# First dense matrix by seven block products per pair of token blocks, its weights' factors made in three steps per unit

## The chip, the cores and the metric

The kernel runs on one core of a Trainium2 chip. The metric is device time in microseconds (us), taken as the median of the runs. The profile is of one execution; its span runs from the first instruction to the last.

## What is computed

Three layers run one after the other, all in fp32: retention (linear attention with decay) over 8 batches, 8 heads and 576 positions; a mixture of 8 experts, one expert for each of the 4608 tokens; and a dense pair of matrices with a squared ReLU between them. The change lies in the third layer and in the making of its weights, which takes place during the second.

```python
def _moe_ref(x, w_gate, w1, w2):            # x: 4608 x 512
    logits = x @ w_gate                     # 512 x 8
    expert_idx = np.argmax(logits, axis=1)
    ...
    for e in range(E):
        mask = expert_idx == e
        h = np.maximum(x[mask] @ w1[e], 0.0)        # 512 x 1024
        out[mask] = gate_w[mask, None] * (h @ w2[e])  # 1024 x 512

def _moe2_ref(x, w_in, w_out):              # w_in 512 x 2048, w_out 2048 x 512
    h = x @ w_in
    r = np.maximum(h, 0.0)
    g = r * r
    return (g @ w_out).astype(np.float32)
```

The dense weights arrive as float64, which the kernel reads as pairs of 32-bit words.

## The kernel before, in words

**Precision.** Every product of the expert and the dense layer is made of three matmuls: each operand is split into a high part (rounded to the TensorE's fp32r format by a ScalarE copy) and a low part (the rest, by a VectorE subtraction), and high x high, high x low and low x high are added up in PSUM.

**Expert stage.** Work goes in 64 units `u = 8 e + f`: expert `e`, slice `f` of 128 hidden features. A unit is `first(u)`, 24 matmuls of 320 token slots in two parts (L712 to L714), each with a ScalarE ReLU into `hh` and a VectorE op into `hl` (L718, L719), and `second(u)`, 15 matmuls of 512 columns (L736 to L738). TensorE runs `first(u+1)` and then `second(u)`. The two parts use three PSUM banks in turn (`l1_ps`). VectorE and ScalarE also split each unit's weights six units ahead (`split_unit`, L97 and L98, on GpSimd for one unit in eight), turn the next expert's gathered tokens (`transp`, L684 to L689), and make the dense weights: `split_wide` reads 512 float64 columns of one dense slice (`craw`), builds the fp32 value with integer ops, splits it into `cw` (two buffers), and two units later SP stores `cw` to the DRAM tensor `wd_d`. 32 such jobs run at five in eight units. At unit 18 `rest_of` branches on whether any expert has more than 640 tokens; the branch is not taken with these inputs.

**End of the expert stage.** The last six units' `second` run tile by tile, and after each tile `finish` scatters its rows to `y_d`, from which `fetch` reads the tokens of dense block 0 again.

**Dense stage.** Nine blocks of 512 tokens. For each block and each of 16 slices of 128 hidden features, `up` is 12 matmuls of 512 columns into one PSUM bank (L937), `squares` is ReLU, square, split (L942 to L948), and `down` is 12 matmuls into four accumulators (L958 to L960). `up` runs two slices ahead of `down`. All 16 slices of weights (`w<-wd_d`) are loaded once and stay in SBUF. Block 0 starts with half a block (256 columns) while its other tokens arrive. The four accumulators leave through four output tiles.

**Order.** Nothing is scheduled automatically: each engine runs its instructions in the order in which the code issues them, and SP issues nearly all DMAs from one queue in order.

Of the kernel before, what the change touches and what calls it, by code (L numbers as in the profile page):

```python
# [19 lines left out]
NT = 36  # L20
NE = 8
# [6 lines left out]
REST = 18  # L28
# [3 lines left out]
GROUPS = [(0, 8), (8, 16), (16, 24), (24, 30), (30, 36)]  # L32

# [4 lines left out]
def body(ctx, tc, att, tab_v, tab_x, masks, wg, ident, pick, cst, wu, wd, out):  # L38
# [80 lines left out]
    def split_wide(j, raw):  # L119
        v, s = divmod(j, 2)  # L120
        low, high = raw[:, :, 0], raw[:, :, 1]
        m = pools["cv_p"].tile([128, 512], F32, tag="cm", name="cm")
        x = pools["cv_p"].tile([128, 512], F32, tag="cx", name="cx")
        t = pools["cv_p"].tile([128, 512], I32, tag="ct", name="ct")
        a = pools["cv_p"].tile([128, 512], F32, tag="ca", name="ca")
# [9 lines left out]
            out=a.bitcast(I32), in0=xi, scalar=-0x40000000, in1=t, op0=ALU.bitwise_and, op1=ALU.bitwise_or  # L135
        )
        vec.tensor_scalar(
            out=m.bitcast(I32), in0=a.bitcast(I32), scalar1=-0x800000, scalar2=None, op0=ALU.bitwise_and
        )
        vec.scalar_tensor_tensor(  # L140
            out=x, in0=low.bitcast(U32), scalar=2.0 ** -52, in1=m, op0=ALU.mult, op1=ALU.mult
        )
        w = pools["cw_p"].tile([128, 2, 512], F32R, tag="cw", name="cw")
        act.activation(out=w[:, 0], in_=a, func=AF.Copy)
        vec.tensor_tensor(out=a, in0=a, in1=w[:, 0].bitcast(F32), op=ALU.subtract)
        vec.tensor_tensor(out=w[:, 1], in0=a, in1=x, op=ALU.add)
        return lambda: sp.dma_start(out=wd_d[v, :, :, 512 * s:512 * s + 512], in_=w.bitcast(F32))

    def load_dense(v, wpool):
        w = wpool.tile([128, 2, 1024], F32R, tag="w", name="w")  # L150
        sp.dma_start(out=w.bitcast(F32), in_=wd_d[v])
        w_q[NE * 8 + v] = w
# [91 lines left out]
    w_q = {}  # L244

# [6 lines left out]
    with ExitStack() as es:  # L252
# [253 lines left out]
        def lead_rows():  # L506
# [18 lines left out]
        raw = {}  # L525
        lead_x = [
            pools["cw_p"].tile([128, 2, 512], F32R, tag="cw", name=f"lead{s}").rearrange(
                "p s (k n) -> p (s k) n", n=128 * LEAD
            ) for s in range(2)
# [30 lines left out]
        for t in range(NT):  # L560
# [39 lines left out]
            if t % 6 == 2 and 12 <= t < 36:  # L600
                w_q[t // 6 - 2] = split_unit(t // 6 - 2, raw.pop(t - 2), pool)
# [4 lines left out]
        for v, tags in ((4, ("ct", "ca")), (5, ("cm", "cx"))):  # L606
            halves[v] = [pools["cv_p"].tile([128, 512], F32, tag=t, name="half") for t in tags]
# [483 lines left out]
```

## Time and profile before

| | before |
|---|---|
| median of 3 runs | 1433.29 us (1427.59 to 1435.78) |
| profiled execution | 1436.04 us, span 1434.2 us |
| PE busy | 97% of the span |
| first dense matmul | at 644.4 us |
| granted clock, mean | 0.991 |

PE is TensorE, DVE VectorE, ACT ScalarE, POOL GpSimd, SP the queue that issues DMAs. A busy PE is a union of overlapping matmuls, so its pace is read from counts over a stretch.

### The profile page before, as it was taken

The page shows a single profiled execution, that of the slowest core. Times are in us where ns is not written, and L with a number is a line of the kernel's source. Part 1 is how long each engine was busy: PE and PEld are TensorE (multiplying, and loading weights), DVE is VectorE, ACT ScalarE, POOL GpSimd, SP SyncE. Part 2 cuts the span into 40 slices and gives each one's busy share as a digit, 9 for nine tenths or more (in the row PEclk, how much of TensorE's full clock was granted, in tenths as well). Part 3 has the DMA queues.
Part 4 walks back from the last instruction along what each step waited for, and adds up shares of the span by engine and source line. Part 5 has one row for each costly group of instructions (what it writes and reads, how often), then busy time and mean ns, then how long its engine had stood idle before and what let it go on. Part 6 is the DMA issues. An engine that isn't in the chain of part 4 may idle for free.

```text
span 1434.2 us, 20323 instructions
## 1 busy us (share of the span) xinstructions
PE 1391.3 (97%) x8217; PEld 1192.2 (83%) x8217; DVE 712.5 (50%) x1187; ACT 435.3 (30%) x764; POOL 313.2 (22%) x277
## 2 busy tenths in 40 slices
PE   7989799998999999999999999999999999999998
PEld 5777688887999999998888888888888888888887
DVE  5667656886888888723323233232333323333222
ACT  1212233443444444422222222222222222222221
POOL 2223246765657557310000000000000000000000
PEclk9999999999999999999999999999999999999999
DMA  8999744765756757538120020200102020020000
GB/s 309 293 298 303 210 131 135 241 226 176 234 186 222 227 185 237 189 134 312 81 59 0 1 59 0 59 1 27 33 0 59 1 57 3 0 59 1 30 0 30
DMA packets 92406, 172.51 MB, mean 120 GB/s; under 512 B 16654, under 2 KB 54030, under 8 KB 86672
## 3 DMA queue, kind: packets, MB, share of 16 engines
q1 hardware_dynamic: 82944, 151.03, 33.3%
q0 software_dynamic: 9360, 20.10, 4.3%
q8 instruction: 66, 1.08, 0.3%
q14 instruction: 36, 0.29, 0.1%
HBM read 125.86 MB, written 46.28 MB: 120 GB/s over the span
## 4 chain that ended last, share of the span: by engine, by line
PE 72%; issue 3%; DMA 1%; POOL 0%; SPq 0%; ACT 0%; POOLq 0%; DVE 0%
PE fl L937 27%; PE fa L959 9%; PE fa L958 9%; PE fa L960 9%; PE l L712 3%; PE l L713 3%; PE l L714 3%; PE acc L737 3%; PE acc L736 3%; PE acc L738 3%; DMA w<-wd_d 1%; DMA y_d<-y,sidx 0%; POOL y_d L227 0%; SPq L633 0%; DMA yi<-y_d 0%
## 5 line engine op out<-in xcount | busy, mean ns | idle before, releaser
L937 PE MATMUL fl<-xt,w 128*128 128x512 f32 (+1 forms) x1776 | 415.3, 383 | 1.5 <-DMA w<-wd_d 1.5
L937 PEld LDWEIGHTS fl<-xt,w 128*128 128x128 f32 x1776 | 327.1, 188 | 67.3 <-issue 1.9
L944 DVE TENSOR_TENSOR fr<-fr 128x512 f32<-128x512 f32 x144 | 99.8, 693 | 401.2 <-ACT fr L942 401.2
L958 PE MATMUL fa<-w,gh 128*128 128x512 f32 x576 | 224.1, 389 | 0.0
L959 PE MATMUL fa<-w,gh 128*128 128x512 f32 x576 | 224.1, 389 | 0.0
L960 PE MATMUL fa<-w,gl 128*128 128x512 f32 x576 | 224.1, 389 | 0.0
L942 ACT ACTIVATE fr<-fl 128x512 f32<-128x512 f32 x144 | 86.2, 599 | 416.0 <-PE fl L937 416.0
L206 POOL DMA_INDIRECT xs<-x_d,qidx x140 | 154.0, 1100 | 44.4 <-issue 42.4
L712 PE MATMUL l<-xt,w 128*128 128x320 f32 (+1 forms) x480 | 150.2, 313 | 8.8 <-DVEq L759 6.2
L713 PE MATMUL l<-xt,w 128*128 128x320 f32 (+1 forms) x480 | 149.8, 312 | 0.0
L948 DVE TENSOR_TENSOR gl<-fr,gh 128x512 fp32r<-128x512 f32 x144 | 99.8, 693 | 100.6 <-ACT gh L946 100.6
L714 PE MATMUL l<-xt,w 128*128 128x320 f32 (+1 forms) x480 | 149.7, 312 | 0.0
L958 PEld LDWEIGHTS fa<-w,gh 128*128 128x128 f32 x576 | 108.1, 188 | 22.5
L959 PEld LDWEIGHTS fa<-w,gh 128*128 128x128 f32 x576 | 108.2, 188 | 22.3
L960 PEld LDWEIGHTS fa<-w,gl 128*128 128x128 f32 x576 | 108.0, 188 | 22.4
L736 PE MATMUL acc<-w,hh 128*128 128x512 f32 x320 | 125.7, 393 | 0.0
L737 PE MATMUL acc<-w,hh 128*128 128x512 f32 x320 | 125.3, 392 | 0.0
L738 PE MATMUL acc<-w,hl 128*128 128x512 f32 x320 | 124.8, 390 | 0.1
L946 ACT ACTIVATE gh<-fr 128x512 fp32r<-128x512 f32 x144 | 91.0, 632 | 109.7 <-DVE fr L944 109.7
L712 PEld LDWEIGHTS l<-xt,w 128*128 128x128 f32 x480 | 90.7, 189 | 12.1 <-issue 6.6
L713 PEld LDWEIGHTS l<-xt,w 128*128 128x128 f32 x480 | 90.7, 189 | 2.4 <-DVE xt L689 0.2
L714 PEld LDWEIGHTS l<-xt,w 128*128 128x128 f32 x480 | 90.7, 189 | 0.0
(140 smaller groups left out, 1511.4 us busy)
## 6 DMA issues: line engine op xcount, KB each, us to landing
raw<-wu SPq DMA_DIRECT2D x62, 512.0 KB, 4.0
in<-att SPq DMA_DIRECT2D x28, 1024.0 KB, 7.9
craw<-wd SPq DMA_DIRECT2D x32, 512.0 KB, 5.6
wd_d<-cw SPq DMA_DIRECT2D x32, 512.0 KB, 6.7
w<-wd_d SPq DMA_DIRECT2D x16, 1024.0 KB, 16.4
x_d<-xr SPq DMA_DIRECT2D x144, 64.0 KB, 5.4
yi<-y_d SPq DMA_DIRECT2D x32, 256.0 KB, 6.0
out<-fo SPq DMA_DIRECT2D x32, 256.0 KB, 2.8
```

What stands on the lines that cost most here:

```text
L206: pool.indirect_dma_start(out=xs, out_offset=None, in_=src, in_offset=bass.IndirectOffsetOnAxis(ap=index, axis=0),)
L712: pe.matmul(ps, w[:, 0, k], hi[:, k, cs], start=(k == 0), stop=False)
L713: pe.matmul(ps, w[:, 0, k], lo[:, k, cs], start=False, stop=False)
L714: pe.matmul(ps, w[:, 1, k], hi[:, k, cs], start=False, stop=(k == 3))
L736: pe.matmul(acc[i], hh[:, cs], w[:, 0], start=(f == 0), stop=False)
L737: pe.matmul(acc[i], hh[:, cs], w[:, 1], start=False, stop=False)
L738: pe.matmul(acc[i], hl[:, cs], w[:, 0], start=False, stop=(f == 7))
L937: pe.matmul(ps, w[:, s, k], x[:, k, ts], start=(n == 0), stop=(n == 11))
L944: vec.tensor_tensor(out=gg, in0=r, in1=r, op=ALU.mult)
L958: pe.matmul(acc[i], gh[:, cs], w[:, 0], start=(f == 0), stop=False)
L959: pe.matmul(acc[i], gh[:, cs], w[:, 1], start=False, stop=False)
L960: pe.matmul(acc[i], gl[:, cs], w[:, 0], start=False, stop=(f == 15))
```

## The change

The dense layer's first matrix is taken in blocks of two by two. Tokens go in pairs of blocks and the 512 input features in two halves of 256, so that each product of a pair with 256 hidden features is four blocks wide, and seven products of half the inner length replace eight. A product `up(T, j, i, n)` is six matmuls instead of two times twelve for a block of 128 features and two token blocks: per pair `T` and per `j` (8 of them, 256 hidden features each) seven products in the order `ORDER` fill three kinds of PSUM bank. Products 7, 3, 2 and 6 add on top of what a bank already holds, and `keep`, `block` and the subtractions in `up` combine the seven. Block 0 is alone, so its two halves form the first pair (`T = 0`, 256 columns per matmul); blocks 1 and 2, 3 and 4, 5 and 6, 7 and 8 form the others (512 columns). All `up` of a pair come first; then `halve` splits the stored squares and `down` runs, one block of the pair after the other.

The left factors (sums of weight blocks, split high and low) are made in the expert stage: per `j` six jobs, one per unit from unit 5 to 52: two `narrow`, two `left_factors`, two `split_wide`. Each job has three steps in its unit: before `first`, after it, and at the start of the next unit. `cw` has one buffer, twice as large. The right factors (sums of token blocks) are made by `factor`, for `T = 0` on VectorE at the start of the dense stage, for later pairs on GpSimd, ScalarE and VectorE during the `down` of the pair before. Weights no longer stay in SBUF: `stream` loads 1 MB tiles of `ws_d` through a ring of four buffers, 22 tiles for `T = 0` and 30 for each other pair. `split_unit` goes to GpSimd for two units in eight. `rest_of` moves from unit 18 to the end of the loop over units.

```diff
+LEFT = [
+    (1, "11", ALU.add, "22"), (2, "21", ALU.add, "22"), (3, "11", None, None), (4, "22", None, None),
+    (5, "11", ALU.add, "12"), (6, "21", ALU.subtract, "11"), (7, "12", ALU.subtract, "22"),
+]
+RIGHT = [
+    (1, "11", ALU.add, "22"), (2, "11", None, None), (3, "12", ALU.subtract, "22"), (4, "21", ALU.subtract, "11"),
+    (5, "22", None, None), (6, "11", ALU.add, "12"), (7, "21", ALU.add, "22"),
+]
+ORDER = [5, 1, 4, 7, 3, 2, 6]
+KEPT = [5, 1, 7, 4, 2, 6, 3]
...
-    pools["cw_p"] = scope(early, "cw_p", 2, side="right")
+    pools["cw_p"] = scope(early, "cw_p", 1, side="right")
...
-    wd_d = dram.tile([NF, 128, 2, 1024], F32, name="wd_d")
+    ws_d = dram.tile([22, 128, 4, 512], F32, name="ws_d")
...
+    def narrow(raw, tag, made):
+        t, m, x = words(raw)
+        yield
+        low_word(raw, m, x)
+        a = pools["cv_p"].tile([128, 512], F32, tag=tag, name=tag)
+        vec.tensor_tensor(out=a, in0=t, in1=x, op=ALU.add)
+        made.append(a)
+        yield
...
+    def split_wide(v, raw):
+
+        t, m, x = words(raw)
+        yield
+        w = pools["cw_p"].tile([128, 4, 512], F32R, tag="cw", name="cw")[:, 0:2]
+        act.activation(out=w[:, 0], in_=t, func=AF.Copy)
+        low_word(raw, m, x)
+        yield
+        vec.tensor_tensor(out=t, in0=t, in1=w[:, 0].bitcast(F32), op=ALU.subtract)
+        vec.tensor_tensor(out=w[:, 1], in0=t, in1=x, op=ALU.add)
+        yield lambda: sp.dma_start(
+            out=ws_d[14 + v // 2, :, 2 * (v % 2):2 * (v % 2) + 2], in_=w.bitcast(F32)
+        )
...
+    def left_factors(j, x0, x1, part):
+
+        blk = {"11": x0[:, 0:256], "12": x0[:, 256:512], "21": x1[:, 0:256], "22": x1[:, 256:512]}
+        these = KEPT[0:4] if part == 0 else KEPT[4:7]
+        n = len(these)
+        yield
+        sums = pools["cv_p"].tile([128, 3, 512], F32, tag="cv", name="sums").rearrange("p a (b n) -> p (a b) n", n=256)
+        w = pools["cw_p"].tile([128, 4, 512], F32R, tag="cw", name="cw").rearrange("p k (s n) -> p k s n", s=2)
+        s = blk[LEFT[these[-1] - 1][1]]
+        act.activation(out=w[:, n - 1, 0], in_=s, func=AF.Copy)
+        for m, i in enumerate(these[:-1]):
+            _, a, op, b = LEFT[i - 1]
+            vec.tensor_tensor(out=sums[:, m], in0=blk[a], in1=blk[b], op=op)
+        act.activation(out=w[:, 0:n - 1, 0], in_=sums[:, 0:n - 1], func=AF.Copy)
+        yield
+        vec.tensor_tensor(out=w[:, n - 1, 1], in0=s, in1=w[:, n - 1, 0].bitcast(F32), op=ALU.subtract)
+        vec.tensor_tensor(
+            out=w[:, 0:n - 1, 1], in0=sums[:, 0:n - 1], in1=w[:, 0:n - 1, 0].bitcast(F32), op=ALU.subtract
+        )
+        k = 7 * j + 4 * part
...
+    stream_of = [t for T in range(5) for t in (*range(14), *(range(14, 22) if T == 0 else 2 * [*range(14, 22)]))]
+
+    def stream(on):
+
+        n = len(ring_q)
+        w = on.tile([128, 4, 2, 256], F32R, tag="w", name="wq")
+        sp.dma_start(out=w.rearrange("p k s n -> p k (s n)").bitcast(F32), in_=ws_d[stream_of[n]])
+        ring_q.append(w)
...
+    def factor(i, x1, x2, hi, lo, cs, on=None):
+
+
+        _, a, op, b = RIGHT[i - 1]
+        blk = {"11": x1 and x1[:, 0:2], "21": x1 and x1[:, 2:4], "12": x2 and x2[:, 0:2], "22": x2 and x2[:, 2:4]}
+        s = blk[a]
+        if b:
+            s = xf_p.tile([128, 2, 128], F32, tag="xs", name="xsum")
+            (on or pool).tensor_tensor(out=s, in0=blk[a], in1=blk[b], op=op)
+        parts = [
+            (h[:, :, cs], l[:, :, cs], s[:, ks])
+            for ks, h, l in zip((slice(0, 2),) if len(hi) == 1 else (slice(0, 1), slice(1, 2)), hi, lo)
+        ]
+        for h, l, s in parts:
+            act.activation(out=h, in_=s, func=AF.Copy)
+
+        def rest():
+            for h, l, s in parts:
+                vec.tensor_tensor(out=l, in0=s, in1=h.bitcast(F32), op=ALU.subtract)
+
+        return rest
...
+        def first_of_them(order, x1, x2):
+            rest = None
+            for i, t in order:
+                r = factor(i, x1[t], x2[t], [x0_c[i, 0]], [x0_c[i, 1]], slice(128 * t, 128 * t + 128), vec)
+                if rest:
+                    rest()
+                rest = r
+            rest()
...
+        work = [(what, j, r) for j in range(8) for what, r in (
+            ("in", 0), ("in", 1), ("sum", 0), ("sum", 1), ("out", 0), ("out", 1))]
...
+            job, rests = None, []
+            if last_job:
+                f_ = next(last_job)
+                if f_:
+                    f_()
+                last_job = None
...
+                rests.append(split_unit(v, raw.pop(v), pool if f in (5, 6) else vec))
+            if 5 <= u < 5 + len(work):
+                what, j, r = work[u - 5]
+                if what == "in":
+                    job = narrow(wide.pop(0), ("ca", "cb")[r], made)
+                elif what == "sum":
+                    job = left_factors(j, *made[2 * j:], r)
+                else:
+                    job = split_wide(2 * j + r, wide.pop(0))
...
+            for f_ in rests[:1]:
+                f_()
+            if job:
+                next(job)
+            for f_ in rests[1:]:
+                f_()
...
+                next(job)
+                last_job = job
...
-                if u == REST:
-                    rest_of()
...
+        rest_of()
+        for _ in range(2):
+            stream(w_a)
...
+                first_factors()
...
+        bank_of = {5: "b5", 1: "b1", 4: "b4", 7: "b1", 3: "b5", 2: "b4", 6: "b5"}
+        bank_ps = {"b1": b1_ps, "b4": b4_ps, "b5": b5_ps}
+        steps = [(None, 0)] + [(2 * n - 1, 2 * n) for n in range(1, 5)]
...
+            terms = [(c, a, b) for c in range(2) for a, b in ((0, 0), (0, 1), (1, 0))]
+            for m, (c, a, b) in enumerate(terms):
+                pe.matmul(
+                    ps, w[:, a, c], xc[T][i, b][c], start=(i in (5, 1, 4) and m == 0), stop=(m == 5),
+                    skip_group_check=True,
+                )
...
+            def block(b, ps, s):
+                o = g[b][:, j, 0:n]
+                if s is None:
+                    act.activation(out=o, in_=ps, func=AF.Relu)
+                    act.activation(out=o, in_=o, func=AF.Square)
+                else:
+                    vec.tensor_tensor(out=o, in0=ps, in1=s, op=ALU.add)
+                    vec.scalar_tensor_tensor(out=o, in0=o, scalar=0.0, in1=o, op0=ALU.max, op1=ALU.mult)
+
+            if i in (5, 1, 4):
+                keep(f"s{i}", j, ps, n)
+                if all((f"s{m}", j) in sums for m in (5, 1, 4)):
+                    vec.tensor_tensor(out=at("s4"), in0=at("s4"), in1=at("s5"), op=ALU.subtract)
+                    vec.tensor_tensor(out=at("s1"), in0=at("s1"), in1=at("s4"), op=ALU.add)
+                    if j in cut and not cut.discard(j):
+                        vec.tensor_tensor(out=at("s1"), in0=at("s1"), in1=bank("b4"), op=ALU.subtract)
...
+            elif i == 7:
+                block("11", ps, at("s4"))
+            elif i == 3:
+                block("12", ps, None)
+            elif i == 2:
+                block("21", ps, None)
+                if ("s1", j) in sums:
+                    vec.tensor_tensor(out=at("s1"), in0=at("s1"), in1=ps, op=ALU.subtract)
+                else:
+                    cut.add(j)
+            else:
+                block("22", ps, at("s1"))
...
+        def halve(T, h, f):
+
+            hi, lo = [pools["cg_p"].tile([128, 512], F32R, tag=f"c{s}", name=f"c{s}") for s in "hl"]
+            if T:
+                parts = [(g["12"[f % 2] + "12"[h]][:, f // 2], slice(0, 512))]
+            else:
+                parts = [(g["12"[f % 2] + "12"[s]][:, f // 2, 0:256], slice(256 * s, 256 * s + 256)) for s in range(2)]
+            for s, o in parts:
+                act.activation(out=hi[:, o], in_=s, func=AF.Copy)
+                vec.tensor_tensor(out=lo[:, o], in0=s, in1=hi[:, o].bitcast(F32), op=ALU.subtract)
+            cg[T, h, f] = hi, lo
...
+                o = pools["cg_p"].tile([128, 512], F32, tag="o", name="fo")
...
+        head = [(0, "up", j, i) for i, j in (
+            (4, 0), (4, 1), (4, 2), (2, 0), (2, 1), (2, 2), (4, 3), (2, 3),
+            (5, 0), (5, 1), (1, 0), (1, 1), (7, 0), (7, 1), (3, 0), (3, 1), (6, 0), (6, 1),
+        )]
+        slots = []
+        for T in range(5):
+            slots += [(T, "up", j, i) for j in range(8) for i in ORDER if (T, "up", j, i) not in head]
+            slots += [(T, "down", h, f) for h in range(2 if T else 1) for f in range(16)]
...
+        for T, _, j, i in head[:8]:
+            up(T, j, i, 256)
+        x2 = [turn(yi[0][:, 2], x0_p)]
+        order = [(5, 0), (1, 0), (7, 0), (5, 1), (1, 1), (7, 1), (3, 0), (3, 1), (6, 0), (6, 1)]
+        first_of_them(order[:3], x0_t, x2)
+        x2.append(turn(yi[0][:, 3], s_p, "s5"))
+        first_of_them(order[3:], x0_t, x2)
+        for T, _, j, i in head[8:]:
...
+                if T < 4 and b == 6 and a in (4, 5):
+                    if a == 4:
+                        load, jobs = prepare(T + 1)
+                    load(a - 4)
...
+                for _ in range(2 if T else 3):
+                    if jobs:
+                        jobs.pop(0)()
+            t = tile_of(T, what, a, b)
+            left[t] -= 1
+            if left[t] == 0 and t >= 4 and t + 4 < len(stream_of):
+                stream(w_a)
         for i in (0, 1, 3, 2):
```

Place 1: ScalarE in the expert stage, over about one unit. `w<-raw` is the high part of a unit's weights, `hh<-l` the ReLU of `first`, `cw` the high part of a dense factor, `cm<-craw` and `cv<-craw` the first step of reading float64. Before:

```order
L126 ACTIVATE cm<-craw 128x512
L144 ACTIVATE cw<-ca 128x512
L97 ACTIVATE w<-raw 128x1024
L718 ACTIVATE hh<-l_5445 128x320
L718 ACTIVATE hh<-l_5460 128x320
L126 ACTIVATE cm<-craw 128x512
L144 ACTIVATE cw<-ca 128x512
```

After:

```order
L808 ACTIVATE hh<-l_3137 128x320
L808 ACTIVATE hh<-l_3152 128x320
L176 ACTIVATE cw<-cv 128x512
L112 ACTIVATE w<-raw 128x1024
L778 ACTIVATE xt_3031<-xf 128x4x128
L140 ACTIVATE cv<-craw 128x512
L808 ACTIVATE hh<-l_3207 128x320
L808 ACTIVATE hh<-l_3222 128x320
L176 ACTIVATE cw<-cv 128x512
```

The copy into `cw` keeps its place behind the two ReLUs, but it now stands in each of four units in six, always on the same buffer.

Place 2: ScalarE where the dense stage begins; `xt` are the token operands' high parts, `fr`/`gh` the squares before, `s` and `g` the kept products and squares after. Before:

```order
L655 ACTIVATE xt_8041<-yf 128x4x128 x2
L747 ACTIVATE y<-acc_7755,gg 128x512
L655 ACTIVATE xt_8041<-yf 128x4x128
L655 ACTIVATE xt_8041<-yf 128x2x128 x2
L942 ACTIVATE fr<-fl_8160 128x512
L946 ACTIVATE gh<-fr 128x512
```

After (the end of the first eight products, and what follows):

```order
L1113 ACTIVATE g_8194<-b_8218 128x256
L1114 ACTIVATE g_8194<-g_8194 128x256
L1085 ACTIVATE s_8225<-b_8251 128x256
L1113 ACTIVATE g_8194<-b_8251 128x256
L1114 ACTIVATE g_8194<-g_8194 128x256
L739 ACTIVATE xt_8142<-yf 128x2x128
L739 ACTIVATE xt_8143<-xsum 128x2x128 x2
```

Before, the copies of the later tokens stand ahead of the first product's ReLU; now the copies of the later tokens (`xt<-yf`, `xt<-xsum`, the last two rows) stand behind all results of the first eight products.

Place 3: SP's queue from the end of the expert stage; `yi` and `yq` are the tokens of the dense blocks. Before:

```order
L151 DMA w<-wd_d 128x2048 x4
L633 DMA yi<-y_d 32x8x128 x4
L633 DMA yi<-y_d 32x4x128 x8
L633 DMA yi<-y_d 32x16x128 x4
L151 DMA w<-wd_d 128x2048 x12
L979 DMA out<-fo 128x512 x4
```

After:

```order
L317 DMA wq<-ws_d 128x2048 x2
L707 DMA yi<-y_d 32x4x128 x16
L317 DMA wq<-ws_d 128x2048 x6
L707 DMA yq<-y_d 32x4x128 x8
L317 DMA wq<-ws_d 128x2048 x2
L707 DMA yq<-y_d 32x4x128 x8
L317 DMA wq<-ws_d 128x2048 x4
```

The twelve loads of weights that stood in one row behind the tokens are now a ring, with the tokens of the next pair between its tiles, eight DMAs at a time.

## Rows read from the trace of the kernel before

**Rows 1.** The page's first part, of the whole span: busy us (share) xinstructions

```profile
PE 1391.3 (97%) x8217; PEld 1192.2 (83%) x8217; DVE 712.5 (50%) x1187; ACT 435.3 (30%) x764; POOL 313.2 (22%) x277
```

**Rows 2.** Windows in the dense stage: PE busy, PEld, DVE, ACT, POOL, clock, DMA share, GB/s

```profile
644.40:650.20 5.80, 5.80 (x50) 5.80 (x49) 2.94 (x6) 2.06 (x4) 0.98 (x1) 1.00 0.16 48
...
663.00:1420.00 757.00, 757.00 (x3340) 627.01 (x3341) 244.28 (x358) 199.15 (x326) 0.00 (x0) 1.00 0.12 35
```

**Rows 3.** Groups by form, PE, whole span: xcount | busy us, mean ns | idle before

```profile
L937 PE MATMUL fl<-xt,w 128*128 128x512 f32 x1680 | 403.6, 389 | 1.5 <-DMA w<-wd_d 1.5
...
L937 PE MATMUL fl<-xt,w 128*128 128x256 f32 x96 | 11.7, 283 | 0.0
```

**Rows 4.** Waits of PE, whole span: total us, times, longest

```profile
PE l L712 <- DVEq L759: 6.2, 1, 6.2
...
PE fl L937 <- DMA w<-wd_d: 1.5, 1, 1.5
```

**Rows 5.** Timeline, PE, one unit of the expert stage: start us, us

```profile
543.87 0.30 PE L712 MATMUL l<-xt,w 128*128 128x320 f32 x1
...
550.81 0.30 PE L712 MATMUL l<-xt,w 128*128 128x320 f32 x1
```

**Rows 6.** Groups by form, DVE, 400 to 600 us

```profile
L98 DVE TENSOR_TENSOR w<-raw,w 128x1024 fp32r<-128x1024 f32 x25 | 30.5, 1220 | 6.7 <-ACT w L97 6.4
L719 DVE SCALAR_TENSOR_TENSOR hl<-l,hh 128x320 fp32r<-128x320 f32 x58 | 26.5, 483 | 7.8 <-ACT hh L718 7.8
...
L127 DVE SCALAR_TENSOR_TENSOR cx<-cm,craw 128x512 f32<-128x512 f32 x18 | 12.4, 687 | 0.6
...
L137 DVE TENSOR_SCALAR cm<-ca 128x512 int32<-128x512 int32 x18 | 7.9, 436 | 0.6
```

**Rows 7.** The same of ACT

```profile
L144 ACT ACTIVATE cw<-ca 128x512 fp32r<-128x512 f32 x18 | 11.4, 635 | 41.5 <-issue 41.5
```

**Rows 8.** Source L147, the store of a dense factor: its last line

```profile
DMA to landing us min/median/max: 3.1/6.7/10.0
```

**Rows 9.** Windows of the twelve loads of dense weights, columns as in rows 2

```profile
665.00:670.00 5.00, 5.00 (x24) 4.13 (x23) 1.39 (x2) 1.23 (x2) 0.00 (x0) 1.00 1.01 419
```

**Rows 10.** Windows at the leftover branch, columns as in rows 2

```profile
326.00:334.00 8.00, 2.04 (x9) 1.34 (x8) 1.63 (x4) 2.35 (x4) 6.02 (x7) 0.78 0.79 248
334.00:340.00 6.00, 5.79 (x28) 5.69 (x29) 3.18 (x5) 1.68 (x4) 4.62 (x5) 0.73 0.48 149
```

**Rows 11.** Timeline, DVE, where the expert stage ends

```profile
641.37 1.31 DVE L648 STREAM_TRANSPOSE yf<-yi 128x512 f32<-128x512 f32 x2
...
648.16 0.77 DVE L648 STREAM_TRANSPOSE yf<-yi 128x256 f32<-128x256 f32 x2 [0.93 <-DMA yi<-y_d]
```

**Rows 12.** Groups by form, DVE, 640 to 1434 us

```profile
L944 DVE TENSOR_TENSOR fr<-fr 128x512 f32<-128x512 f32 x144 | 99.8, 693 | 401.2 <-ACT fr L942 401.2
...
L656 DVE TENSOR_TENSOR xt<-yf,xt 128x256 fp32r<-128x256 f32 x2 | 0.8, 422 | 0.2 <-ACT xt L655 0.2
```

**Rows 13.** The same of ACT

```profile
L946 ACT ACTIVATE gh<-fr 128x512 fp32r<-128x512 f32 x144 | 91.0, 632 | 109.7 <-DVE fr L944 109.7
...
L655 ACT ACTIVATE xt<-yf 128x256 fp32r<-128x256 f32 x2 | 0.7, 417 | 2.1 <-DVE yf L648 2.1
```

**Rows 14.** Timeline, SP's queue, dense stage

```profile
741.53 2.71 SPq L633 DMA_DIRECT2D yi<-y_d  x4
```

**Rows 15.** DMA issues, whole span: xcount, KB each, median us to landing

```profile
out<-fo SPq DMA_DIRECT2D x32, 256.0 KB, 2.8
...
yi<-y_d SPq DMA_DIRECT2D x8, 64.0 KB, 2.0
```

**Rows 16.** Timeline, DVE, beside a GpSimd split

```profile
411.10 0.69 DVE L689 TENSOR_TENSOR xt<-xf,xt 128x512 fp32r<-128x512 f32 x1 [0.70 <-ACT xt L688]
...
415.26 1.92 DVE L689 TENSOR_TENSOR xt<-xf,xt 128x512 fp32r<-128x512 f32 x1 [0.70 <-ACT xt L688]
```

**Rows 17.** Timeline, POOL, the same stretch

```profile
414.23 2.40 POOL L98 TENSOR_TENSOR w<-raw,w 128x1024 fp32r<-128x1024 f32 x1 [3.63 <-ACT w L97]
```

More of the change, by code (lines that the diff above doesn't have):

```diff
@@ L27 @@
 FIN = 6
-REST = 18
 LEAD = 2
@@ L140, in split_wide, with low_word @@
+    def low_word(raw, m, x):
         vec.scalar_tensor_tensor(
-            out=x, in0=low.bitcast(U32), scalar=2.0 ** -52, in1=m, op0=ALU.mult, op1=ALU.mult
+            out=x, in0=raw[:, :, 0].bitcast(U32), scalar=2.0 ** -52, in1=m, op0=ALU.mult, op1=ALU.mult
         )
[L143 to L146, printed above, removed]
@@ L600, in body @@
             if t % 6 == 2 and 12 <= t < 36:
-                w_q[t // 6 - 2] = split_unit(t // 6 - 2, raw.pop(t - 2), pool)
+                split_unit(t // 6 - 2, raw.pop(t - 2), pool)()
         for f in late:
@@ new lines, in body, with weights, keep @@
+        bank_ps = {"b1": b1_ps, "b4": b4_ps, "b5": b5_ps}
+        steps = [(None, 0)] + [(2 * n - 1, 2 * n) for n in range(1, 5)]
+        xc, cg, pt, acc = {}, {}, {}, {}
+        first_of = [0] + [22 + 30 * n for n in range(4)]
+        left = {}
+        def weights(n, k):
+            return ring_q[n][:, k]
+        sums, half, cut = {}, {}, set()
+        def keep(name, key, ps, n):
+            if n < 512 and key % 2 and (name, key - 1) in half:
+                s = half.pop((name, key - 1))[:, 256:512]
+            else:
+                s = s_p.tile([128, 512], F32, tag=name, name=name)
+                if n < 512:
+                    half[name, key] = s
+            sums[name, key] = s
+            act.activation(out=s[:, 0:n], in_=ps, func=AF.Copy)
@@ L954, in down @@
+        def down(T, h, f, tiles=range(4)):
+            hi, lo = cg[T, h, f]
+            w = ring_q[first_of[T] + 14 + 8 * h + f // 2][:, 2 * (f % 2):2 * (f % 2) + 2].rearrange("p k s n -> p k (s n)")
             for i in tiles:
@@ new lines, in tile_of @@
+        def tile_of(T, what, a, b):
+            return first_of[T] + ((7 * a + KEPT.index(b)) // 4 if what == "up" else 14 + 8 * a + b // 2)
+        for m in slots:
+            left[tile_of(*m)] = left.get(tile_of(*m), 0) + 1
+        for n in range(2):
+            stream(w_a)
[4 more added lines that the diff above has]
+        first_of_them(order[:3], x0_t, x2)
@@ new lines, in body @@
+        x2.append(turn(yi[0][:, 3], s_p, "s5"))
+        first_of_them(order[3:], x0_t, x2)
+        for T, _, j, i in head[8:]:
+            up(T, j, i, 256)
+        jobs = []
+        for m, (T, what, a, b) in enumerate(slots):
+            if (T, what, a, b) == (0, "up", 3, 5):
+                late_es.close()
+                places_es.close()
+                pools["cg_p"] = scope(es, "cg_p", 3, reuse="tile")
+                xe_p = scope(es, "xe_p", 1, reuse="tile")
+            for s in slots[m + 2:m + 3] + (slots[m + 1:m + 2] if what == "up" else []):
+                if s[1] == "down" and (s[0], *s[2:]) not in cg:
+                    halve(s[0], *s[2:])
+            if what == "up":
+                up(T, a, b, 512 if T else 256)
+                if T < 4 and b == 6 and a in (4, 5):
+                    if a == 4:
+                        load, jobs = prepare(T + 1)
+                    load(a - 4)
+            elif m < len(slots) - 2:
+                if (a, b) == (0, 0) and T == 0:
+                    x_v.extend(places_of_factors())
+                down(T, a, b)
+                if b == 15:
+                    store(T, a)
+                for _ in range(2 if T else 3):
[4 more added lines that the diff above has]
+            if left[t] == 0 and t >= 4 and t + 4 < len(stream_of):
+                stream(w_a)
@@ L1009, in body @@
         for i in (0, 1, 3, 2):
-            for s in steps[-2:]:
-                down(*s, [i])
-            store(NB - 1, [i])
+            for T, _, h, f in slots[-2:]:
+                down(T, h, f, [i])
+            store(T, h, [i])
 def _tokens(a):
```

300 lines of the change are left out of this document (153 added, 147 removed).

## The prediction

> **What bounds the kernel now.** I read the page's engine shares first: PE is busy for 1391.3 us, 97% of the span, every other engine for half of it or less [rows 1]. The windows say whether that is work or overlap: from 663 to 1420 us PE starts 3340 matmuls of 512 columns in 757.0 us without a gap, at a granted clock of 1.00, so one costs 0.2266 us [rows 2] (the 389 ns of its group is its length, neighbours overlapping [rows 3]). The waits of PE for the dense weights and for the leftover branch come to 1.5 and 6.2 us in all [rows 4]. So the dense stage is a count of matmuls, and the expert stage too: its units start 6.94 us apart [rows 5]. Fewer matmuls are worth their price, if the work that feeds them stays under PE. The sum is made on the profiled execution, 1436.0 us, which lies 2.7 above the median.
>
> **Gain in `up`.** Before: 1680 matmuls of 512 columns and 96 of 256, 1680 x 0.2266 + 11.7 = 392.4 us [rows 3]. After: four pairs x 8 `j` x 7 products x 6 = 1344 of 512 columns, 304.6 us, and 336 of 256 columns for `T = 0` at 11.7 / 96 = 0.122, 41.0 us. **-46.9 us**. `down` is unchanged.
>
> **One `cw` buffer in the expert stage.** A round of six units now writes `cw` in four: two "sum" jobs (1 MB and 0.75 MB) and two "out" jobs (0.5 MB). Place 1 of the order shows the copy behind the ReLUs of `first`, and SP's store in the next unit; the next job's copy must wait until that store has landed. Behind that copy on ScalarE stand `split_unit`'s copy and the next ReLUs `hh<-l`, which free the banks that `first` writes: a late copy is a late PE. An "out" job holds the buffer for a copy of 0.64 us [rows 7], two subtractions of 0.69, as L127 [rows 6], and the landing L. A "sum" job holds it for the copies (1.0 to 1.25), the subtractions (0.42 + 1.26, the latter by L98's 1.22) and its larger store, L + 0.6 to 1.25. Added along a round, the buffer is free at 12 + 3 L us after the first copy, where the fourth copy wants it after three units less about 0.6 us of product, 21 us; so it comes 3 L - 9.4 late. Into that goes some 1.6 us more for VectorE standing at its own work ahead of the split, and out of it 4.1: the three banks let a ReLU be 4 us late (needed 5.6 us after its product, normally there at 1.6). PE then loses about 3 L - 12 us per round, eight rounds, and about 8 us where the units with gates and `finish` meet it. What is L? The trace's stores of 0.5 MB landed in 3.1 / 6.7 / 10.0 us [rows 8], but each stood behind 1 MB of raw weights and `craw`, 2.5 us at the 419 GB/s that a full queue reached [rows 9]; without it the median is 4.2. With 3.1 there is no loss in the rounds (0 to 8 us in all), with 3.6 8, with 4.2 13, with 5 32, with 6.7 about 70. I take the 4.2, because the store is now issued at a unit's start, where the raw loads of the unit are just being asked for: **+14**, bounds 0 and 33 (of L = 5, between the two). The Trainium skill, "DMA: Bandwidth & Descriptors", "Anatomy of one DMA — SWDGE (gpsimd) path", gives a DMA 2.0 us plus its bytes over 436 GB/s (for GpSimd's queue; here SP issues): an estimate of 3.2 us for 0.5 MB. The fastest row, 3.1, agrees, the median does not. By that figure the term would be 0 to 8 us and the whole 1403 to 1411.
>
> VectorE's own load rises in these units from 2.69 to 3.34 us of jobs; the heaviest (an "out" with a token turn and both `hl`) comes to 7.9 against 6.94, a lateness under the 4.1 that the banks allow; no price. More of `split_unit` on GpSimd relieves it.
>
> **Start of the dense stage.** Now 8 of `T = 0`'s products stand ahead, each 6 x 0.122 = 0.73 us. Two waits. First, SP: ring tiles 0 to 5 come early, tile 6 stands behind the tokens' DMAs (place 3) and is issued when the last scatters are done, near 646 us; it lands some 4.1 us later (the fastest 1 MB by 419 GB/s and a small DMA's 2.0 [rows 9, 15]), where PE wants it at 644.5 + 6 x 0.73 = 648.9: 1.5 us. Second, ScalarE (place 2): the later tokens' copies stand behind the ReLU and square of those eight products. The tokens themselves are there at 648.2 [rows 11]; PE is out of ready products at about 650.4. Then: last product's ReLU and square 0.76, transposes 0.8 [rows 11], copies and subtractions of 0.42 each [rows 12, 13], three factors of them in a chain before the first of the next products, and more before the second: 4.9 us of PE idle in all. A PE idle that long gives back clock: in the branch's stretch, after 6 us with 2.04 busy of 8, 28 matmuls took 5.8 us at 0.73 [rows 10]; full speed would be about 3.3, so +2.5. Less 1.5, the old first wait for weights [rows 4]. **+7.4** (1 to 12).
>
> **Products of `T = 0`.** For `j` = 2 and 3, products 4 and 2 lie in the head, so 1 and 7, and 3 and 6, stand next to each other and share a bank: PE waits about 0.65 us for keep and subtraction between, four times, +2.6. Tile 12 stands on SP behind eight `yq` of 0.68 us each [rows 14], 5.4 us; the 14 tiles, 14.7 MB in 41 us, want 358 GB/s of 419 [rows 9], so a late issue is not made up: +2.7. **+5.3** (0 to 10).
>
> **`T = 0`'s `down`s.** Beside 16 slots of 2.72 us, VectorE has `halve` (0.84), three jobs of `factor` per slot: subtractions (about 1.2) and transposes (0.53), and GpSimd sums of about 0.7 x 1.9 = 1.3 us each. VectorE's two-input ops slow down beside GpSimd: L689 took 0.69 us alone, and 1.92 when GpSimd's split ran from 414.23 to 416.63 [rows 16, 17]. 2.6 us of VectorE plus part of 1.3 in each 2.72 makes `halve` late at times: **+3** (0 to 9). For later pairs two jobs per slot and a slack of two slots hide it.
>
> **Small.** Three output tiles per pair's boundary: the fourth accumulator waits for the first `out` (2.8 us [rows 15]), 0.3 us in each of four pairs, **+1.3**. The leftover branch moves: its 6.2 us and slow stretch go from unit 18 to where `finish` ends, **0** (-4 if PE has stopped there anyway for the first dense tokens, +4 if first loads come behind it). `keep`, `block` and the subtractions are VectorE and ScalarE work of 0.4 to 0.7 us an op (L944 0.69 [rows 12], L946 0.63 [rows 13]) in products of 1.36 us; about 1.1 us per product on VectorE, hidden.
>
> **Sum:** -46.9 + 14 + 7.4 + 5.3 + 3 + 1.3 + 0 = -15.9: 1420.1 for the profiled execution, 1417.4 on the median. I forecast 1418, and for this case alone 1406 to 1430.
>
> **Rivals.**
> *A. The covers hold.* Stores land as the fastest row (3.1), VectorE keeps up: `cw` costs about 3, the start 5, the rest 5: 1433.3 - 46.9 + 13 = 1399. For it: 0.5 MB at 419 GB/s is 1.25 us, so most of L is a fixed part. Against: the store shares the queues with 1 MB of loads in each unit.
> *B. Slower: the single buffer takes the gain.* If stores land late as before, L = 5.5, each of eight rounds loses 4.5 us, and 8 more: 44, with the other terms (17) 1433.3 - 46.9 + 61 = 1447 to 1450. It decides from 46.9 - 17 = 29.9 us of loss on, that is L = 4.9. For it: the median of rows 8 as it stands is 6.7; against: its queue ahead.
> *C. GpSimd blocks VectorE wherever they meet.* 87 more GpSimd ops (80 sums, 7 splits). If each holds a VectorE op for its whole length, `T = 0`'s `down`s lose 9 where I took 3, and about 1 us is lost at each of some 8 places, later `down`s and units of the expert stage, that find no slack: 1417.4 + 6 + 8 = 1431. Rows 16 and 17 show that it can: the op that met the split ended only after it. The Trainium skill, "SBUF — State Buffer", "Who interferes with whom", states it as an exclusive lock: a VectorE op with two SBUF inputs and a GpSimd op that reads SBUF exclude each other for a whole instruction, whichever starts first. The 1.92 us agrees.
>
> **How the numbers follow.** Forecast 0.50, A 0.22, B 0.18, C 0.10. The range is 1393 to 1441: below it lies a part of A in which the start costs nothing as well (0.08), above it B's worse half (0.12). 0.5% is 7.2 us, which is about what a measurement here can tell from no change. Faster than 1426.1: all of A (0.22), 0.43 of the forecast's 0.50, 0.03 each of B and C, 0.71. Within: 0.07 of the forecast, 0.07 of C, 0.03 of B, 0.17. Slower than 1440.5: B's rest, 0.12.
>
> **What would show it.** PE's count must fall by only 96, from 8217 to 8121 (1776 in `up` become 1680, 336 of them of half width), and a window over a later pair's `up`s show 0.2266 us each with no idle. Waits of ScalarE for a `cw` store, with PE's wait for `hh<-l` or for its bank behind them, show the second term: expected in units "sum 1" to "out 1", 1 to 2 us in a round, none in the two "in" units; first dense matmul near 644 + 14. PE's waits where tokens are `x0` operands, and a clock below 1 there, show the third; DVE waits beside POOL sums in 690 to 740 us the fifth. The forecast is wrong if the units with `cw` start 6.94 us apart (A), if they lose over 4 us a round (B), if a pair's products wait on `keep` or `block` for more than the 0.4 to 0.7 us I gave, or if the ring falls behind in later pairs, which want 193 GB/s.

## The result and the profile after

The changed kernel took 1442.99 us (median of 20 runs) against 1435.22 us before (20 runs as well, the first three of them those of the table ahead): ratio 1.0059, interval 1.0043 to 1.0076. It is 0.6% slower, where 1418 was forecast. The profiled execution has a span of 1438.5 us, 4.3 more than before.

In 13 of the 17 runs of the experiments TensorE lost another 67 to 94 us to waits shown as "issue" in slices 3 to 6 of the experts, for a cause that stays open, and the kernel before took 1549 to 1553 us beside them instead of 1433 to 1435: these runs are called disturbed, and of them only ratios and stretches outside those slices are read.

TensorE's share and the windows of a later pair (its `up`s, then its `down`s; columns as in [rows 2]):

```profile
PE 1360.4 (95%) x8121; PEld 1165.2 (81%) x8121; DVE 848.7 (59%) x1518; ACT 532.2 (37%) x1053; POOL 385.4 (27%) x364
...
942.25:1018.41 76.16, 76.16 (x337) 63.08 (x336) 37.30 (x56) 34.15 (x58) 0.00 (x0) 1.00 0.65 220
1018.41:1105.45 87.04, 87.04 (x385) 72.09 (x384) 42.27 (x81) 31.85 (x72) 15.69 (x20) 1.00 0.63 220
```

TensorE lost 31 us of busy time and the whole gained nothing. The pair runs as forecast: 336 matmuls in 76.16 us, 0.2267 each, no idle, and all four pairs take the same 76.16. The gain is there; it was spent elsewhere. Where, the waits of TensorE say (total us, times, longest), beside [rows 4]:

```profile
PE l L802 <- DVE hl L809: 29.6, 17, 4.9
...
PE b L1099 <- ACT s L1085: 7.9, 5, 6.1
...
PE b L1099 <- ACT xt L739: 4.0, 1, 4.0
PE b L1099 <- DMA wq<-ws_d: 2.5, 1, 2.5
```

The first line is the expert stage, the others are `T = 0`'s products. Two places, then. Before, the wait for `hl` was small:

```profile
PE l L712 <- DVE hl L719: 2.6, 3, 1.1
```

ScalarE does wait for the stores of `cw`, as the prediction's second term has it, but in the expert stage no wait of TensorE names ScalarE:

```profile
ACT cw L176 <- DMA ws_d<-cw: 23.9, 7, 4.6
ACT cw L194 <- DMA ws_d<-cw: 20.2, 8, 4.7
```

**The expert stage.** The starts of `first` in TensorE's timeline give each unit's length. From unit 8, the first of expert 1, to unit 58, units take 10.5 us over 6.94 each in all before (7.8 of them at the branch), and 37.6 after, though the branch is no longer there. Most of that, 27.3 us, is lost where one expert ends and the next begins, in slices 7 and 0: 8.85 and 10.86 us (units 23, 24), 9.36 and 10.25 (31, 32), 11.60 and 10.80 (47, 48), where [rows 5] have 6.94. (The expectations below count these units four too high: their twelfth unit is unit 8, and their fourth and fifth slices are slices 7 and 0.) VectorE at units 22 to 24, from the timeline (start, length, what):

```profile
351.61 0.43 DVE L151 TENSOR_SCALAR cv<-cv 128x512 int32<-128x512 int32 x1
351.95 3.48 DVE L779 TENSOR_TENSOR xt<-xf,xt 128x512 fp32r<-128x512 f32 x1
355.36 0.88 DVE L809 SCALAR_TENSOR_TENSOR hl<-l,hh 128x320 fp32r<-128x320 f32 x2
...
358.70 2.77 DVE L180 TENSOR_TENSOR cw<-cv 128x512 fp32r<-128x512 f32 x1
361.40 0.70 DVE L774 STREAM_TRANSPOSE xf<-xs 128x512 f32<-128x512 f32 x1
```

GpSimd in the same stretch:

```profile
352.47 2.40 POOL L114 TENSOR_TENSOR w<-raw,w 128x1024 fp32r<-128x1024 f32 x1
358.39 2.53 POOL L114 TENSOR_TENSOR w<-raw,w 128x1024 fp32r<-128x1024 f32 x1 [3.52 <-ACT w L112]
```

and TensorE waiting:

```profile
355.89 0.41 PE L802 MATMUL l<-xt,w 128*128 128x320 f32 x1 [1.65 <-DVE hl L809]
...
366.74 0.42 PE L802 MATMUL l<-xt,w 128*128 128x320 f32 x1 [3.64 <-DVE hl L809]
```

Two ops of 0.7 us took 3.48 and 2.77: each ended 0.55 us after GpSimd's split (which ended at 354.87 and 360.92), as in [rows 16, 17]. Before, this happened once in an expert and cost 1.2 us. Now it happens in two units running, and `hl`, queued behind on VectorE, is late: in all 17 of TensorE's waits for `hl`, VectorE had been busy until that op began. From 230 to 640 us, 13 VectorE ops took over one and a half times the median of their kind, and each ended 0.07 to 0.56 us after a GpSimd split; together they are 26.4 us over their medians, against 9.9 in seven ops before. TensorE's longest wait for `hl`, in unit 8, follows two splits that ran one right after the other:

```profile
236.74 4.71 POOL L114 TENSOR_TENSOR w<-raw,w 128x1024 fp32r<-128x1024 f32 x2
...
237.12 4.88 DVE L141 SCALAR_TENSOR_TENSOR cv<-cv,craw 128x512 f32<-128x512 f32 x1 [1.26 <-ACT cv L140]
...
244.64 0.64 PE L802 MATMUL l<-xt,w 128*128 128x320 f32 x1 [4.87 <-DVE hl L809]
```

**`T = 0`'s products** took 63.06 us (669.61 to 732.67), not 41.0. ScalarE and GpSimd at the start:

```profile
671.66 0.38 ACT L1085 ACTIVATE s<-b 128x256 f32<-128x256 f32 x1 [0.32 <-PE b L1099]
679.44 0.38 ACT L1085 ACTIVATE s<-b 128x256 f32<-128x256 f32 x1 [7.40 <-DMA y_d<-y,sidx]
```

```profile
673.59 0.98 POOL L289 DMA_INDIRECT y_d<-y,sidx  x1 [5.98 <-DMA yi<-y_d]
```

The third `keep` waits 7.4 us for the last scatter of the expert stage: a wait that no line of the code names. The clock follows (windows, columns as before):

```profile
675.60:681.60 6.00, 1.72 (x8) 1.72 (x9) 0.00 (x0) 1.80 (x6) 0.00 (x0) 0.78 0.48 191
681.60:687.60 6.00, 2.86 (x12) 2.27 (x11) 1.32 (x4) 2.98 (x8) 0.00 (x0) 0.50 0.00 0
687.60:693.60 6.00, 4.67 (x24) 4.50 (x24) 5.66 (x15) 3.22 (x9) 0.00 (x0) 0.58 0.00 0
```

After an idle of 6 us the granted clock is 0.50, the lower level, and half-width matmuls cost 0.244 us instead of 0.122.

### The profile page after: what moved, and what is told of

It reads as the page before. It is cut to its first block, busy times and chain, and to the rows that moved or that the text cites. A ratio compares the mean times of both kernels' runs of the same rounds, so it can differ in the third digit from the quotient of the medians.

```text
span 1438.5 us, 21519 instructions
## 1 busy us (share of the span) xinstructions
PE 1360.4 (95%) x8121; PEld 1165.2 (81%) x8121; DVE 848.7 (59%) x1518; ACT 532.2 (37%) x1053; POOL 385.4 (27%) x364
## 4 chain that ended last, share of the span: by engine, by line
PE 55%; DMA 12%; DVE 12%; POOL 9%; issue 8%; ACT 4%; SPq 1%; DVEq 0%; ACTq 0%; POOLq 0%
PE b L1099 23%; PE fa L1161 8%; PE fa L1162 8%; PE fa L1163 8%; POOL xs L268 7%; DMA in<-att 5%; DMA ws_d<-cw 2%; DMA y_d<-y,sidx 2%; PE x L437 1%; DMA xs<-x_d,qidx 1%; DVE cv L141 1%; PE sc L385 1%; POOL y_d L289 1%; DVE hl L809 1%; PE x L433 1%
## 5 line engine op out<-in xcount | busy, mean ns | idle before, releaser
L1099 PE MATMUL b<-xt,wq 128*128 128x512 f32 (+1 forms) x1296 | 269.6, 366 | 15.4 <-ACT s L1085 7.9
L1099 PEld LDWEIGHTS b<-xt,wq 128*128 128x128 f32 x1296 | 224.4, 192 | 55.6 <-ACT s L1085 9.0
L1161 PE MATMUL fa<-wq,ch 128*128 128x512 f32 x576 | 225.1, 391 | 3.5 <-DVE fo L1173 1.6
L1163 PE MATMUL fa<-wq,cl 128*128 128x512 f32 x576 | 224.4, 390 | 0.0
L1162 PE MATMUL fa<-wq,ch 128*128 128x512 f32 x576 | 224.3, 389 | 0.0
L1151 DVE TENSOR_TENSOR cl<-g,ch 128x512 fp32r<-128x512 f32 (+1 forms) x160 | 107.3, 680 | 178.0 <-ACT ch L1150 175.8
L1150 ACT ACTIVATE ch<-g 128x512 fp32r<-128x512 f32 (+1 forms) x160 | 91.1, 583 | 161.7 <-PE fa L1162 161.5
L1161 PEld LDWEIGHTS fa<-wq,ch 128*128 128x128 f32 x576 | 108.1, 188 | 28.2 <-ACT ch L1150 3.0
L1163 PEld LDWEIGHTS fa<-wq,cl 128*128 128x128 f32 x576 | 108.1, 188 | 23.3 <-DVE cl L1151 1.1
L1162 PEld LDWEIGHTS fa<-wq,ch 128*128 128x128 f32 x576 | 108.2, 188 | 22.3
L802 PEld LDWEIGHTS l<-xt,w 128*128 128x128 f32 x480 | 91.0, 190 | 36.6 <-DVE hl L809 34.0
L803 PEld LDWEIGHTS l<-xt,w 128*128 128x128 f32 x480 | 91.2, 190 | 2.4 <-DVE xt L779 0.2
L1099 PE MATMUL b<-xe,wq 128*128 128x512 f32 x384 | 92.3, 389 | 0.0
```

The source lines that it names most:

```text
L802: pe.matmul(ps, w[:, 0, k], hi[:, k, cs], start=(k == 0), stop=False)
L803: pe.matmul(ps, w[:, 0, k], lo[:, k, cs], start=False, stop=False)
L1099: pe.matmul(ps, w[:, a, c], xc[T][i, b][c], start=(i in (5, 1, 4) and m == 0), stop=(m == 5), skip_group_check=True,)
L1151: vec.tensor_tensor(out=lo[:, o], in0=s, in1=hi[:, o].bitcast(F32), op=ALU.subtract)
L1161: pe.matmul(acc[i], hi[:, cs], w[:, 0], start=(f == 0), stop=False)
L1162: pe.matmul(acc[i], hi[:, cs], w[:, 1], start=False, stop=False)
```

## The experiments

Three theories. **G**: VectorE ops blocked behind GpSimd's splits cost the expert stage its time. **C**: the one `cw` buffer does (the prediction's second term). **W**: the start of the dense stage waits for the memory under the last scatter.

**1. Splits, buffer and branch, first attempt** (disturbed). The comments name the runs: e1 leaves one split on GpSimd, e2 none, e3 gives the "out" jobs a buffer of their own and leaves the branch out, e3b leaves out the branch alone.

```diff
-                rests.append(split_unit(v, raw.pop(v), pool if f in (5, 6) else vec))
+                rests.append(split_unit(v, raw.pop(v), pool if f == 6 else vec))   # e1
+                rests.append(split_unit(v, raw.pop(v), vec))                       # e2
```

```diff
-        w = pools["cw_p"].tile([128, 4, 512], F32R, tag="cw", name="cw")[:, 0:2]
+        w = pools["cw_p"].tile([128, 2, 512], F32R, tag="co", name="co")           # e3
...
-        lp = scope(es, "lp", 1, reuse="tile")                                      # e3, e3b
...
-        rest_of()                                                                  # e3, e3b
```

> GpSimd makes the low part of a unit's weights in one unit of eight, as before the change, not in two. Theory G (a VectorE op that meets GpSimd's split stands until the split ends, and two neighbouring units of that leave no slack): VectorE's long ops between 230 and 640 us fall from 13, with 28 us above the median of their kind, to about 6 with 10; TensorE's wait for hl falls from 29.6 us to 15 or less; the time falls by 10 to 15 us, to about 1430. Theory C (the one cw buffer: ScalarE waits 44 us for its store): VectorE has 1.2 us more per expert, nothing is gained, 1441 to 1448.

> GpSimd makes no low part in the units with jobs; VectorE makes all of them (1.22 us each, 16 more than now... two in each of seven experts). Theory G: no VectorE op between 230 and 640 us is blocked any more, TensorE's wait for hl falls below 12 us, the expert stage loses 20 us less and the time is about 1423, unless VectorE is now too full in the units with a token turn, when it is that of one split, 1430. Theory C: ScalarE's waits for the cw store stay at 44 us and the time at 1440 to 1450.

> The out jobs write a buffer of their own, so that of the four copies of a round only two can meet a store that is under way; for the room that it takes, the leftover branch (not taken with these inputs) is left out. Theory C: ScalarE's waits for the cw store fall from 44 us to about 20, TensorE's wait for hl from 29.6 to about 12, the time by some 18 us more than in the kernel that only leaves the branch out. Theory G: ScalarE's waits fall as well, but TensorE's wait stays within 5 us of 29.6 and the time within 4 us of that kernel's.

> Only the leftover branch (not taken with these inputs) is left out, as the yardstick for the run with a second buffer. It stands where the last units' second begins and TensorE waits 1.8 us there: 1 to 3 us faster than the changed kernel, 1441, the expert stage otherwise the same. If the branch costs what it cost in its old place (6.2 us and a slow stretch), 6 to 9 us faster.

Ratios to before, in this order: 0.9929 (0.9883 to 0.9975), 0.9972 (0.9913 to 1.0030), 0.9935 (0.9894 to 0.9975), 0.9913 (0.9867 to 0.9959); once more each, also disturbed: 0.9908, 0.9897, 0.9991, 0.9951, with intervals of 0.004 to 0.013 to either side. These ratios do not tell the edits apart, so no time follows for G, C or the branch. Two things can be read. VectorE's ops over one and a half times their median are, over the whole expert stage, 20.6 to 22.4 us over it in 13 or 14 ops with two splits, 10.1 and 11.5 in seven with one, and none are left with no split. Slices 7 and 0, outside the disturbance, lose 16.3 and 14.3 us with the branch alone left out, 13.6 and 14.0 with a second buffer as well, 5.8 and 5.3 with one split, 1.9 and 1.4 with none. That favours G over C, but the runs of 2, with the same two splits, lose 5.3, 18.5 and 5.1 there, so single profiles scatter.

**2. The start of the dense stage** (disturbed).

```diff
-        g_p = scope(es, "g_p", 1, reuse="tile")
         s_p = scope(es, "s_p", 2, reuse="tile")
+        g_p = scope(es, "g_p", 1, reuse="tile")
```

```diff
-        for T, _, j, i in head[:8]:
+        for T, _, j, i in head[:4]:
             up(T, j, i, 256)
         x2 = [turn(yi[0][:, 2], x0_p)]
...
         first_of_them(order[:3], x0_t, x2)
+        for T, _, j, i in head[4:7]:
+            up(T, j, i, 256)
         x2.append(turn(yi[0][:, 3], s_p, "s5"))
-        first_of_them(order[3:], x0_t, x2)
+        first_of_them(order[3:5], x0_t, x2)
+        for T, _, j, i in head[7:8]:
+            up(T, j, i, 256)
+        first_of_them(order[5:], x0_t, x2)
```

> The pool of kept products is opened before the pool of squares, so that no tile that the first products write lies on the y rows of the last scatter. Theory W (ScalarE's third keep waits 7.4 us for the end of that scatter, since its tile lies in the same memory): ScalarE's wait for y_d goes, the first eight products run through, TensorE's 6.1 us wait for s goes and with it the stretch at half clock; T = 0's products take 52 to 54 us instead of 63 and the time falls by 9 to 11 us, to 1433. Rival (the later tokens' copies bound the start in any case): TensorE's wait for xt grows from 4.0 by as much, and the time falls by under 4 us.

> Only the order in which ScalarE and VectorE are given the later tokens' factors is changed: they stand between the results of the first eight products, not behind them. Theory W: the third keep still waits for the scatter, to about the same moment, so only the 4.0 us wait of TensorE for xt shrinks, to about 1: 2 to 4 us faster than the changed kernel, 1440. Rival (the copies' place is what delays the start, as the prediction's third term has it): 7 us faster, 1436.

> Both of the two: pools opened in the other order, and the later tokens' factors between the results of the first eight products. T = 0's products take 48 to 50 us instead of 63, no TensorE wait over 2.5 us is left there but the one for the ring's twelfth tile (2.5), the clock stays at 1.00, and the time is 13 to 15 us less, 1429. If the waits only move to another tensor: 1434 to 1438.

Ratios to before: 0.9884 (0.9821 to 0.9948), 0.9847 (0.9761 to 0.9934), 0.9866 (0.9768 to 0.9963), again too close to tell apart. `T = 0`'s products, from TensorE's timeline: 63.8 to 67.9 us in the eight runs of 1, which leave this place alone, with a median of 64.5; 60.2 with the pools exchanged, 60.0 with the order alone, 55.1 with both (52.7 to 55.6 in the runs below that have both). Where the pools are exchanged, ScalarE no longer waits for `y_d`, so W holds; but TensorE's waits of that kernel show where half of its gain went:

```profile
PE b L1099 <- DMA wq<-ws_d: 5.8, 2, 3.2
...
PE b L1099 <- ACT xt L739: 4.0, 1, 4.0
```

The ring tile behind the tokens on SP (2.7 us) and the later tokens' copies (4.0) are next in line, and the clock still falls to 0.50. With the order alone the wait for `s` stays (6.3 us) and that for `xt` goes. Each edit is worth some 4.4 us by one profile each, half of what W said of the first; together 9.4, where 13 to 15 were expected. With both, TensorE still waits 2.4 and 3.7 us for tiles of the ring, and the clock behind the first of these waits is 0.78.

**3. All three edits**: both of 2, and no split on GpSimd.

> As the last, and VectorE makes all weights' low parts, GpSimd none. Theory G (VectorE ops blocked behind GpSimd's split cost the expert stage its time): the expert stage is 15 to 22 us shorter than in the run before it, the total about 1411. Theory C (the one cw buffer): the same time as the run before it or up to 5 us more, 1429 to 1434.

> The same kernel as the run with all three edits (pools in the other order, the later tokens' factors between the first results, no split of weights on GpSimd), on another chip if there is one, where the kernel before takes about 1435 us again. Theory G: no VectorE op of the expert stage blocked, units 6.94 us apart where the changed kernel lost 4 to 8 us per expert at the fourth and fifth slices, about 1412 us. Theory C: the same losses in those units from ScalarE's waits for the cw store, about 1430 us.

The first fell on a disturbed run (0.974, 0.965 to 0.983). The second: **1412.45 us** against 1432.79, ratio 0.9852 (0.9828 to 0.9877): theory G's time, though 14.9 us are still lost in units 8 to 58, where G had every unit at 6.94. It is faster than both kernels. The 14.9 stand for 37.6 in the changed kernel (5.3 for 27.3 in slices 7 and 0), while ScalarE's waits for the store are as they were there (23.9 and 20.2):

```profile
ACT cw L176 <- DMA ws_d<-cw: 26.2, 8, 5.5
ACT cw L194 <- DMA ws_d<-cw: 19.6, 8, 4.3
...
PE l L802 <- DVE hl L809: 12.0, 9, 2.5
```

**4. The split alone**, the one word of e2.

> Only the splits move from GpSimd to VectorE. Where the kernel before takes 1435: Theory G 1420 (23 us under the changed kernel, as the units of the run with all three edits give), Theory C 1440 or more. The T = 0 products stay at 63 to 65 us.

1423.05 us against 1434.53, ratio 0.9921 (0.9891 to 0.9951); units lose 12.5 us (5.4 in slices 7 and 0), `T = 0`'s products still take 64.75. One word makes the slower kernel the faster one.

```profile
PE l L802 <- DVE hl L809: 10.9, 10, 2.0
```

**5. A buffer of its own for the "out" jobs**, in the kernel of 3 (and its branch left out, which is not taken). A disturbed run came first: 0.9803 (0.9723 to 0.9884).

> All three edits and a buffer of their own for the out jobs (the leftover branch, not taken with these inputs, left out for the room). Where the kernel before takes 1435: if the one cw buffer is what is left of the expert stage's loss, under 5 us lost over 6.94 per unit from the twelfth on (14.9 with all three edits), 1400 us; if VectorE's own load is, 12 to 15 us lost and 1409 to 1411.

1414.80 us against 1434.53, 0.9848 (0.9802 to 0.9893), and 15.7 us still lost in the units:

```profile
PE l L802 <- DVE hl L809: 15.2, 10, 4.2
...
ACT cw L194 <- DMA ws_d<-cw: 19.6, 8, 4.5
...
ACT co L176 <- DMA ws_d<-co: 10.8, 4, 3.4
```

ScalarE waits 30 us instead of 46 for the stores, and TensorE no less for `hl`: the waits that went had cost it nothing that shows.

**6. Less work for VectorE**, in the kernel of 3.

```diff
-        low_word(raw, m, x)
...
-        vec.tensor_tensor(out=t, in0=t, in1=w[:, 0].bitcast(F32), op=ALU.subtract)
-        vec.tensor_tensor(out=w[:, 1], in0=t, in1=x, op=ALU.add)
+        vec.tensor_tensor(out=w[:, 1], in0=t, in1=w[:, 0].bitcast(F32), op=ALU.subtract)
```

(and in `narrow` one one-input op in place of two.)

> The kernel with all three edits, which leaves out the low 32 bits of the float64 weights: VectorE has 0.9 us less in each in job and 1.4 less in each out job, all DMAs and buffers as they were. If VectorE's own load is what is left: the units from the twelfth on lose under 5 us instead of 14.9, and the time is 1402 to 1405. If it is something else (the tokens' gather, the cw store): 11 us or more still lost, 1410 to 1413.

1400.90 us against 1433.34, 0.9768 (0.9714 to 0.9823); the units lose 2.4 us. ScalarE still waits 32 us for the stores:

```profile
PE l L799 <- DVE hl L806: 5.7, 3, 3.8
...
ACT cw L191 <- DMA ws_d<-cw: 17.6, 8, 2.7
ACT cw L175 <- DMA ws_d<-cw: 14.6, 6, 5.0
```

Beside 5, where the waits for the stores were the same and 15.7 us were lost, this leaves the store no part in the loss, and C falls. What was left was VectorE's own load, in the units where a job meets a token turn or an expert's end: in the kernel of 3 the six longest units (12, 24, 32, 36, 44, 48) took 7.9 to 11.3 us, and VectorE was busy for 7.7 to 10.7 of them.

## Why the prediction was wrong

In short: the expert stage lost 34.9 us where 14 were forecast, and not by the step that was priced. The single `cw` buffer, priced at 14, cost nothing that shows; the splits on GpSimd and VectorE's own load, priced at nothing there, cost about 35.

**What bounds the kernel, the gain, the pairs**: right. 0.2267 us a matmul in the pairs, 304.6 us for them, no wait on `keep` or `block` there; PE's count fell to 8121.

**One `cw` buffer, +14: the step that failed.** The landing was right (4.2 taken, median 4.1 measured), and ScalarE does wait for it (44 us in 15 places). What failed is "a late copy is a late PE": with 15 us of those waits gone nothing was gained (5), and with 32 still there only 2.4 were lost (6). ScalarE is busy for two fifths of that stage (167 of 410 us), so it has room to catch up. The units' loss grew by 34.9 us (37.6 less 10.5, and the branch's 7.8 that had left), of which the split on GpSimd is 22.7 (37.6 to 14.9 in 3; 25.1 by 4) and VectorE's load about 12.5 (14.9 to 2.4). Nor do the term's parts add up: two "sum" jobs and an "out" job, three times L aside, make some 9.5 us as listed, not 12, and by its own list a landing of 4.2 gives 13, not 14.

**"More of `split_unit` on GpSimd relieves it": wrong in sign.** I had the rows that show the block [rows 16, 17], made it rival C, and priced it at `T = 0`'s `down`s and at 1 to 2 us here. The Trainium skill, "SBUF — State Buffer", "Who interferes with whom", has it as an exclusive lock held for a whole instruction: the trace agrees with 3.48 and 2.77 us for ops of 0.7. The first of the two began 0.52 us before the split and was held all the same. An op moved off VectorE saves it 1.22 us and costs it up to 2.8 when they meet.

**VectorE's load, "a lateness under the 4.1 that the banks allow; no price"**: wrong by 12.5. The heaviest unit was put at 7.9 us of VectorE; where GpSimd is no longer in the way, units 36 and 44 have 8.6 and 8.7 and unit 12 has 10.7, and take 9.0 to 11.3 us.

**Start, +7.4, and products, +5.3**: together 22.1 measured, where 14.2 were forecast before the old wait of 1.5 is taken off. The stalls at shared banks (four of 0.47) and at the twelfth tile (2.5) are near the forecast, so the rest, some 18 us for 8.9, is the start. The chain of copies was there (4.0 us of wait); the wait on the scatter's memory (6.1) was not foreseen, and behind the two of them the clock stood at 0.5.

**`T = 0`'s `down`s, +3**: 46.38 us for 43.5, 2.9. The size agrees, the cause is not shown: TensorE's waits there are 1.0 us, for ScalarE's copy in `halve`, and a GpSimd sum took 0.79 us, not 1.3. **Boundaries, +1.3**: 1.9, all at the last pair and not 0.3 at each, so the size is luck. **Branch, 0**: its 7.8 us left the units, and from unit 59's `first` to the dense stage it takes 40.2 us instead of 38.0, so -5.6, by the profiles alone. Without the branch that stretch took 38.1 to 38.6 us in six profiles, with it 39.6 or more; the times of those runs do not settle it.

The sum of these, -46.9 + 34.9 - 5.6 + 22.1 + 2.9 + 1.9, is 9.3; less 3.8 and 0.2 that the changed profile is ahead at the first unit and gains by unit 8, and less the old wait of 1.5 [rows 4], it is 3.8, against 4.3 between the two spans. The measured time lies near rival B's, but for another reason: what happened is rival C's mechanism, in the units of the expert stage.

## What to carry to other kernels

A stage that is bound by one engine's count still has a second engine with slack; before adding work there, add up that engine's queue for the fullest units, not for the mean. Work moved from VectorE to GpSimd can come back to VectorE as blocked time where their ops meet: look for ops whose length is several times the median of their kind. A new tile may lie on memory that an old transfer still reads, and the order in which pools are opened decides which tile it is.

## What the runs showed of the hardware

- A VectorE op with one input was held as well: in the changed kernel the integer `TENSOR_SCALAR` of L151, usually 0.43 us, once took 2.75 beside a split, while GpSimd's own splits kept to 2.35 to 2.53.

```profile
413.93 2.75 DVE L151 TENSOR_SCALAR cv<-cv 128x512 int32<-128x512 int32 x1
...
413.99 2.40 POOL L114 TENSOR_TENSOR w<-raw,w 128x1024 fp32r<-128x1024 f32 x1
```

- A stall costs again in the matmuls that follow it: behind the waits of 6.1 and 4.0 us at the start of the dense stage, 42 matmuls took 2.93 + 1.65 + 4.88 = 9.5 us at a granted clock of 0.5 to 0.6, where 42 at 0.122 are 5.1.
